# First four blocks in pairs with 384-byte load rows, headwise key-query products, late bias sum, fewer weight buffers

## Chip, cores, metric

One core of a Trainium2 chip. The metric is the device time of one execution in microseconds, median of several runs; every time is that of fast or undisturbed runs. TensorE is PE in the profile (PEld its weight loads), VectorE DVE, ScalarE ACT, GpSimd POOL, and SP the engine that issues the loads and stores.

## The reference, cut to what matters

```python
# gated linear attention; q, k, v, f_logit are 4 x 8 x 768 x 48 in float32
f = 1 / (1 + exp(-f_logit))
for t in range(S):
    state = f[:, :, t, :, None] * state + einsum('bhd,bhe->bhde', k[:, :, t], v[:, :, t])
    y[:, :, t] = einsum('bhd,bhde->bhe', q[:, :, t], state)
# y becomes x (3072 x 384), then a feed-forward layer with softplus
h = x @ w_in                                   # w_in  384 x 2048
g = maximum(h, 0) + log1p(exp(-abs(h)))
out = g @ w_out                                # w_out 2048 x 384
```

## The kernel before

The 3072 tokens are 24 blocks of 128. Per block: attention in chunk form (`zz`, `cs`, `ee`, `qkp`, `qkT`, `pp`, `ptm`, `uu`, `oo`, `xx`, `xT`), then `hh` = w_in times `xT`, exp and ln on ACT (`uexp`, `gg`), then `ops` = w_out times `gg`. Weights come in four quarters each, are cast to bf16, half on DVE and half on POOL.

Each piece of work is a task with an engine, an assumed cost, needs and perhaps a buffer. A list order walks through assumed time, picks the task that can start first, and writes it to its engine's queue. Each engine then works through its queue in that order.

```python
def in_order(tasks, slots):
    ...
        for e, waiting in queue.items():           # every engine, "DMA" and "SP" among them
            for t in waiting[:60]:                 # sorted by key
                r = ready(t)                       # None while a need or its buffer has no end yet
                ...
                if first is None or start < first[0] - 0.03:
                    first = (start, t)
...
    def load_w(n, w):
        ... t = work.tile([128, KT, WQ], FP32, name="w32", tag="w32", bufs=8)
...
    turn = blocks(0, 1, 2, 3) + [("wi", w) for w in range(4)] + [("wo", w) for w in range(4)]
    for kd, (n, i) in enumerate(turn):             # then the loads of blocks 4 on
        if n in SRC:
            task(("go", n, i), "SP", 0.5, [(used[n], i - LOADS)], kd, load, (n, i))
            task(("dma", n, i), "DMA", 1.04, [("go", n, i)], kd)
        else:
            task(("go", n, i), "SP", 0.5, [], kd, load_w, (n, i), "w32",
                 [("cast", n, i, 1), ...])         # the buffer is free after this cast
            task(("dma", n, i), "DMA", 2.3, [("go", n, i)], kd)
```

Two assumptions are to be kept in mind. An issue holds SP for 0.5 us whatever the transfer takes; and "DMA" takes its waiting transfers by key, that is in the order of `turn`, not in the order of issue.

Until about 24 us of assumed time, idle stretches of TensorE are filled with dummy matmuls (`ops<-negU,ident`), counted from the assumed start of the next real one.

```python
        each = 0.11 if start < WARM_FROM + 4 else 0.056
        for _ in range(int(max(0.0, start - idle_from - 0.1) / each * 0.9)):
            nc.tensor.matmul(...)                  # dummy
```

## Time and profile before

| | before |
|---|---|
| median of runs | 199.06 us (198.86 to 200.39) |
| span of the profiled run | 197.0 us |
| first `hh` | 24.72 us |
| w_out casts on DVE | 31.7, 34.2, 36.3, 38.4 us |
| TensorE without gaps from | 88 us |

The lines themselves stand in the prediction.

### The profile page before, as it was taken

The numbers are of one execution on the slowest core, as the hardware profiler recorded it, in microseconds if no ns is written. First come the engines' busy times: TensorE is split into PE (matmuls) and PEld (weight loads), VectorE is DVE, ScalarE is ACT, GpSimd is POOL, SyncE is SP. The second block draws the span as 40 slices with busy tenths as digits, with TensorE's granted clock in tenths as the row PEclk, the third lists the DMA queues.
The fourth block names the chain that finished last, engine by engine and source line by source line (L and its number), as shares of the span: only waits on it lengthen the run. The fifth ranks groups of instructions, "written<-read, shape, count | busy, mean of one in ns | idle before, by whom it ended". The sixth has DMA issues, their size and how long they took to land.

```text
span 197.0 us, 6209 instructions
## 1 busy us (share of the span) xinstructions
PE 184.4 (94%) x2491; PEld 152.7 (78%) x2491; DVE 142.9 (73%) x336; ACT 150.1 (76%) x251; POOL 98.1 (50%) x142
## 2 busy tenths in 40 slices
PE   6886997899999999989999999999999999999993
PEld 5775786666687888868888888888888888888872
DVE  6543774625999989999989889858778988773011
ACT  4566388886859996987989797898879778766770
POOL 2266867999997652652463364344246334500000
PEclk9999999999999999999999999999999999999998
DMA  6999999999999999999978757846541101102676
GB/s 124 188 189 176 352 382 374 244 198 187 188 165 194 186 190 173 277 195 208 233 146 172 144 118 160 161 113 137 113 90 41 42 2 43 40 29 75 163 188 171
DMA packets 109532, 32.34 MB, mean 164 GB/s; under 512 B 101184, under 2 KB 107968, under 8 KB 109504
## 3 DMA queue, kind: packets, MB, share of 16 engines
q1 hardware_dynamic: 109504, 31.96, 78.4%
q8 instruction: 19, 0.31, 0.7%
q14 instruction: 9, 0.07, 0.1%
HBM read 27.23 MB, written 4.72 MB: 162 GB/s over the span
## 4 chain that ended last, share of the span: by engine, by line
PE 57%; DVE 12%; SPq 10%; POOL 8%; DMA 6%; ACT 3%; issue 2%; ACTq 0%; POOLq 0%
PE hh L407 22%; PE ops L427 21%; SPq L140 8%; DMA w<-in_moe_w_out_dram 6%; POOL wsum L213 4%; PE qkT L268 3%; PE pp L303 3%; DVE ptm L315 3%; DVE ect L336 2%; POOL w_out_bf L191 2%; SPq L177 2%; PE oo L379 2%; DVE osb L458 1%; PE xTp L393 1%; PE ops L434 1%
## 5 line engine op out<-in xcount | busy, mean ns | idle before, releaser
L407 PE MATMUL hh<-xT,w_in_bf 128*128 128x128 bf16 x1152 | 112.3, 219 | 1.6 <-ACT uexp L415 0.9
L427 PE MATMUL ops<-w_out_bf,gg 128*128 128x384 bf16 x368 | 107.8, 326 | 1.0 <-POOL w_out_bf L191 0.9
L407 PEld LDWEIGHTS <-w_in_bf 128*128 128x128 bf16 x1152 | 88.0, 98 | 22.5 <-DVE xT L191 0.9
L415 ACT ACTIVATE uexp<-hh 128x512 f32<-128x512 f32 x96 | 56.5, 596 | 24.9 <-PE hh L407 24.1
L421 ACT ACTIVATE gg<-uexp 128x1024 bf16<-128x1024 f32 x48 | 50.7, 1056 | 1.4
L427 PEld LDWEIGHTS <-gg 128*128 128x128 bf16 x368 | 35.2, 98 | 5.3 <-issue 1.5
L363 POOL TENSOR_TENSOR sst<-tt,ect 48x192 bf16<-48x192 f32 x32 | 16.5, 517 | 31.7 <-DVE tt L354 25.5
L315 DVE TENSOR_TENSOR ptm<-pp,mask 128x512 bf16<-128x512 f32 x48 | 31.0, 684 | 1.6 <-PE pp L303 1.2
L250 POOL TENSOR_TENSOR qkp<-kk,ee 128x384 bf16<-128x384 f32 x23 | 21.1, 917 | 21.7 <-ACT ee L242 14.1
L191 DVE COPY qkT<-qkT 128x512 bf16<-128x512 bf16 x41 | 17.4, 423 | 13.8 <-PE qkT L268 9.6
L254 POOL TENSOR_TENSOR qkp<-qq,ee 128x384 bf16<-128x384 f32 x24 | 22.2, 924 | 0.3
L336 DVE STREAM_TRANSPOSE ect<-ee 32x128 bf16<-32x128 bf16 x64 | 19.5, 305 | 1.5
L191 POOL CAST vb<-vv 128x384 bf16<-128x384 f32 x24 | 12.6, 524 | 15.5 <-DMA vv<-in_v_dram 10.7
L229 ACT ACTIVATE ff<-ff 128x384 f32<-128x384 f32 x24 | 12.2, 516 | 7.0 <-DMA ff<-in_f_logit_dram 7.0
L454 DVE TENSOR_TENSOR osb<-ops,bias_bc 128x384 f32<-128x384 f32 x16 | 8.9, 556 | 9.4 <-PE ops L427 9.1
L618 PE MATMUL ops<-negU,ident 128*128 128x128 bf16 x169 | 13.9, 233 | 1.9 <-POOL ident masks.py:199 1.9
L213 POOL TENSOR_TENSOR wsum<-wsum,w 128x384 f32<-128x384 f32 x14 | 14.5, 1034 | 0.5
L191 DVE CAST xx<-oo 128x384 bf16<-128x384 f32 x21 | 11.7, 556 | 4.2 <-PE oo L379 3.9
L618 PEld LDWEIGHTS <-ident 128*128 128x128 bf16 x169 | 11.3, 105 | 4.4 <-issue 1.9
L242 ACT ACTIVATE ee<-cs 128x384 bf16<-128x384 f32 x24 | 11.5, 479 | 3.2 <-PE uu L323 1.7
L268 PE MATMUL qkT<-ident,qkp 128*128 128x128 bf16 x160 | 12.7, 219 | 1.0 <-POOL qkp L254 1.0
L303 PE MATMUL pp<-qbd,qkT 112*128 112x256 bf16 x80 | 12.9, 272 | 0.0
(60 smaller groups left out, 201.9 us busy)
## 6 DMA issues: line engine op xcount, KB each, us to landing
ff<-in_f_logit_dram SPq DMA_DIRECT2D x24, 192.0 KB, 4.5
kk<-in_k_dram SPq DMA_DIRECT2D x24, 192.0 KB, 4.4
qq<-in_q_dram SPq DMA_DIRECT2D x24, 192.0 KB, 4.2
vv<-in_v_dram SPq DMA_DIRECT2D x24, 192.0 KB, 4.4
out_dram<-osb SPq DMA_DIRECT2D x23, 192.0 KB, 2.4
w<-in_moe_w_in_dram SPq DMA_DIRECT2D x4, 768.0 KB, 8.6
w<-in_moe_w_out_dram SPq DMA_DIRECT2D x4, 768.0 KB, 12.7
rows<-in_q_dram SPq DMA_DIRECT2D x1, 1152.0 KB, 7.3
```

Source lines behind the costliest of these rows:

```text
L191: on[eng].tensor_copy(out=out, in_=in_)
L213: nc.gpsimd.tensor_tensor(out=wsum, in0=wsum, in1=t[:, j, :], op=ALU.add)
L250: on[eng].tensor_tensor(out=qkp_bufs[i % 3][:, H:2 * H, 0:D], in0=in_t.pop(("k", i)), in1=e_bufs[i % 2][:, H:2 * H, 0:D], op=ALU.mult)
L254: on[eng].tensor_tensor(out=qkp_bufs[i % 3][:, 0:H, 0:D], in0=in_t.pop(("q", i)), in1=e_bufs[i % 2][:, 0:H, 0:D], op=ALU.mult)
L303: nc.tensor.matmul(out=ps[:, u * 256:(u + 1) * 256], lhsT=qkT_t[i][0:112, NP + p, :], rhs=qbd_bufs[i % 2][0:112, p, :], start=True, stop=True,
L315: nc.vector.tensor_tensor(out=to, in0=p_ps.pop((i, half)).rearrange("p (a t) -> p a t", t=128), in1=mask4, op=ALU.mult)
L336: nc.vector.transpose(out=t[32 * r:32 * r + 32], in_=e[96:128, 0:NP, 32 * r:32 * r + 32])
L407: nc.tensor.matmul(out=h_ps[i, j // 4][:, j % 4, :], lhsT=w_in_bf[:, r, j * 128:(j + 1) * 128], rhs=xT_t[i][:, r, :], start=(r == 0), stop ...
L415: nc.scalar.activation(out=u_t[i, a // 2][:, 4 * (a % 2):4 * (a % 2) + 4, :], in_=h_ps.pop((i, a)), func=AF.Exp, bias=0.0, scale=1.0)
L421: nc.scalar.activation(out=g_t[i][:, 8 * a:8 * a + 8, :], in_=u_t.pop((i, a)), func=AF.Ln, bias=0.5, scale=0.5)
L427: nc.tensor.matmul(out=o_ps[i][:, 0:DM], lhsT=g_t[i][:, j, :], rhs=w_out_bf[:, j, :], start=(j == 0), stop=(j == NJ - 1), skip_group_check ...
L618: nc.tensor.matmul(out=idle_ps[:, 0:128], lhsT=ident, rhs=negU, start=True, stop=True, skip_group_check=True)
```

## The change

Its intent: longer load rows for the first four blocks so that the weights arrive sooner; fewer DVE copies; POOL freed of the bias sum while it is needed. The pairs and the 16 output buffers take SBUF, so the weights get five buffers in place of eight.

```diff
     def load(n, i):
+        if i < PAIRED:                       # PAIRED = 4; two tokens per partition
+            t = work.tile([128, H, 2, D], FP32, name=n + "2", tag=n + "2", bufs=2)
+            nc.sync.dma_start(out=t, in_=SRC[n][b, :, c * T:(c + 2) * T, :].rearrange(
+                "h (p e) d -> p h e d", e=2))
...
-            t = work.tile([128, KT, WQ], FP32, name="w32", tag="w32", bufs=8)
+            t = work.tile([128, KT, WQ], FP32, name="w32", tag="w32", bufs=5)
...
+    def a_cs2(i, e):                         # two matmuls, split sum
+    def a_p2(i, e, b):                       # 8 matmuls 48x64 x 48x128, four times a pair
+    def a_u2(i, n): ...                      # halved contractions
+    def a_o2(i, n): ...
...
-    def a_p(i, half):                        # 2 matmuls of 112 rows, 256 columns (qbd)
+    def a_p(i, b):                           # 4 matmuls of 48 rows, 128 columns, in all blocks
...
-        osb = work.tile([128, DM], FP32, name="osb", tag="osb", bufs=6)
+        osb = work.tile([128, DM], FP32, name="osb", tag="osb", bufs=16)
-        nc.vector.tensor_tensor(out=osb_t[i], in0=osb_t[i], in1=bias_bc, op=ALU.add)
+        nc.gpsimd.tensor_tensor(out=osb_t[i], in0=osb_t[i], in1=bias_bc, op=ALU.add)
...                                           # test loads in store() removed
-            task(("go", n, i), "SP", 0.5, [(used[n], i - LOADS)], kd, load, (n, i))
-            task(("dma", n, i), "DMA", 1.04, [("go", n, i)], kd)
+            task(("go", n, i), "SP", 0.55,
+                 [(used[n], i - LOADS) if i - LOADS >= PAIRED else None], kd, load, (n, i))
+            task(("dma", n, i), "DMA", 1.55 if i < PAIRED else 1.05, [("go", n, i)], kd)
...
-                 [("cast", n, i, 1), ("sum", 4 * i + 2) if n == "wo" else None])
+                 [("cast", n, i, 0), ("cast", n, i, 1), ("sum", 4 * i + 2) if n == "wo" else None])
...
-        task(("sum", n), "POOL", 0.91, [...], 40 + 3 * n, add_w, (w, j))
+        task(("sum", n), "POOL", 1.08, [...], SUMS + 8 * n, add_w, (w, j))
-    slots = dict(..., qkp=3, vb=3, qbd=2, w32=8, osb=6)
+    slots = dict(..., qkp=4, vb=4, qkT2=3, w32=5, osb=16)
```

## The prediction

> **What bounds the kernel now.** I read the page's engine shares first, then a table of busy time by stage, then the timelines of TensorE, the DMA-issuing queue and VectorE, and last what TensorE waited for.
>
> ```profile
> span 197.0 us, 6209 instructions
> ...
> PE 184.4 (94%) x2491; PEld 152.7 (78%) x2491; DVE 142.9 (73%) x336; ACT 150.1 (76%) x251; POOL 98.1 (50%) x142
> ...
> PE 57%; DVE 12%; SPq 10%; POOL 8%; DMA 6%; ACT 3%; issue 2%; ACTq 0%; POOLq 0%
> ```
>
> PE at 94% is not useful work: matmuls overlap, and 169 of them are dummies that keep the clock up before the real work. So I count real work by the distance between starts. In unbroken runs 24 `hh` matmuls take 1.34 us (0.0556 each), 8 `ops` 1.30 (0.163 each), and one block's attention needs transposes 0.45, `pp` 0.44, `oo` 0.37, `uu` 0.17, `xTp` 0.17, `cs` 0.16. By stage:
>
> ```profile
> 0.00:24.72 24.72, 19.27 (x303) 16.70 (x304) 13.98 (x38) 12.57 (x25) 13.21 (x26) 1.00 1.09 207
> 24.72:33.00 8.28, 6.99 (x122) 6.29 (x118) 5.65 (x10) 7.01 (x12) 5.06 (x7) 1.00 1.04 380
> 33.00:54.30 21.30, 19.97 (x210) 14.50 (x210) 12.30 (x25) 16.93 (x29) 20.69 (x24) 1.00 1.24 215
> 54.30:88.00 33.70, 32.62 (x456) 27.39 (x456) 32.04 (x79) 28.72 (x49) 21.05 (x31) 1.00 1.08 197
> 88.00:173.00 85.00, 85.00 (x1159) 71.04 (x1160) 71.98 (x172) 71.16 (x120) 38.14 (x57) 1.00 0.54 115
> ```
>
> The columns are stretch, length, busy PE, PEld, DVE, ACT, POOL, then clock, DMA share, GB/s. Four regimes: no `hh` at all until 24.72; POOL nearly full (20.7 of 21.3) until 54; DVE nearly full (32.0 of 33.7) until 88; then PE alone, with no gap. The first stage is set by the loads:
>
> ```profile
> 6.00:12.00 6.00, 5.29 (x94) 4.55 (x91) 3.76 (x10) 2.99 (x7) 3.11 (x5) 1.00 1.42 188
> 21.00:36.00 15.00, 13.23 (x211) 11.24 (x209) 10.00 (x18) 10.36 (x16) 11.00 (x14) 1.00 1.04 372
> ...
> 178.25:178.50 0.25, 1.00 1.08 292
> 178.50:178.75 0.25, 1.00 1.15 321
> ```
>
> ```profile
> 12.98 2.22 SPq L140 DMA_DIRECT2D kk<-in_k_dram  x1
> ...
> 16.87 3.62 SPq L177 DMA_DIRECT2D w<-in_moe_w_in_dram  x4
> ...
> 23.19 0.69 DVE L191 CAST w_in_bf<-w 128x768 bf16<-128x768 f32 x1 [0.50 <-DMA w<-in_moe_w_in_dram]
> ...
> 24.72 1.50 PE L407 MATMUL hh<-xT,w_in_bf 128*128 128x128 bf16 x24
> ```
>
> Sixteen loads of 192-byte rows go ahead of the weights at 188 GB/s, 1.04 us each; weights with long rows then run at 372. The first weight quarter is cast at 23.19 and `hh` starts when both halves are cast. Block 0's `xT` had been ready since 14.2, so weights, not attention, start the feed-forward part. The two lines from 178 us (stretch, length, clock, DMA share, GB/s) are a small load of 384-byte rows that the old kernel happens to make near its end.
>
> What TensorE then waited for (24.7 to 90):
>
> ```profile
> PE qkT L268 <- POOL qkp L254: 1.0, 3, 0.5
> PE hh L407 <- ACT uexp L415: 0.9, 2, 0.7
> PE ops L427 <- POOL w_out_bf L191: 0.9, 3, 0.3
> PE hh L407 <- DVE xT L191: 0.6, 1, 0.6
> ```
>
> **What the Trainium skill says.**
> - "DMA: Bandwidth & Descriptors", Specifications, wants rows of at least 512 B for line rate, and its section on small descriptors names a fixed cost per descriptor. The trace agrees: 188 GB/s at 192 B, 372 at 1.5 to 2 KB, about 300 at 384 B.
> - "TensorEngine Tiling (Array Packing)", Key Properties: tiles of the array work independently, but changing the tiling mode drains it. The trace shows both: eight K=48 `pp` matmuls start about 27 ns apart, but the next full-array matmul comes 0.35 us after the first.
> - "Perfetto Trace Analysis", Optimizing Scalar/DVE Operations: each vector instruction pays a fixed access cost, more from PSUM, so fewer and larger ones help. Here `qkT` copies of 384 and 512 columns take 351 and 423 ns (the first is `xT`): 72 ns per 128 columns, so over 130 ns are fixed.
> - "SBUF — State Buffer", Who interferes with whom: VectorE and GpSimd block each other on a shared port. Here the `w_out_bf` cast on DVE takes 0.56 us alone and up to 1.23 beside POOL's sums.
>
> **The change part by part.**
>
> 1. *Pairs for blocks 0 to 3, 384-byte rows.* Eight loads of 384 KB in place of sixteen of 192 KB. Estimate of one: per engine a 192-byte descriptor takes 16.2 ns (1.04 us over 64) and a 2,048-byte one 88 ns (372 GB/s over 16), so a line through both gives 23.6 ns at 384 B, 1.51 us a load; the small load near the end ran at about 300 GB/s, 1.31 us. I take 1.41: 11.3 us against 16.6. The weights arrive 5.3 us earlier, and `hh` starts at about 19.4 if `xT` of block 0 is there. It should be: the first `ff` pair lands 0.7 us later than now (4.5), four activations of 0.52 to 6.6, `cs` and four exponentials of 0.48 to 9.0, the second `qkp` on POOL to 10, transposes and a wide eviction to 11.5, products and four masks of 0.68 to 14.6, then `oo`, `xx`, `xTp`, `xT` to about 16.5. So the path is −5.3.
>    The pairs add PE work (two-matmul `cs`, 32 products in place of 16, halved contractions in `uu` and `oo`): some 1.3 us a pair. For pair 0 this lies in idle time; of pair 1 I put +1.2 on the path, since more of it now comes after `hh` starts.
> 2. *Headwise products everywhere.* For 20 blocks the three `qkT`/`qbd` copies and the k copy (start to start 0.34 + 0.42 + 0.46 + 0.34 = 1.56 us) become one of 1,024 columns, estimated 423 + 4 × 72 = 711 ns. DVE: −0.85 × 20 = −17 us of busy time, but on the path only where DVE set the pace, 54 to 88. On PE, four matmuls of 256 columns (0.44) become eight of K=48 (0.35 with the drain behind; a drain ahead may add 0.1): −0.1 to 0 per block, −1.0 in all.
> 3. *Bias sum late.* The 15 sums of about 1.03 us leave POOL's stretch from 33 to 49.5, where the timeline shows 4.23 us of them directly before block 4's first `qkp` at 45.28; the casts of `w_out` no longer queue behind them. The seven adds on DVE (0.6 us each, 4.2) go, and 13 adds of about 1 us come to POOL late, where it is under half busy.
> 4. *The lost TensorE time.* Work from 24.72 to the end: 1152 × 0.0556 + 368 × 0.163 + 2.65 (last halves) + 33.9 (attention of 20 blocks, fewer `uu` and state products in first and last chunks) + 0.9 + 0.6 (bias) = 162.1. PE's last matmul starts its end at 193.57, so 168.85 − 162.1 = 6.7 us are lost, nearly all before 88 (the four waits above, 3.4, and the pipeline refill behind each gap). Parts 2 and 3 remove the waits on POOL and DVE: I take −3.0. The ACT waits stay: one block's `exp` and `ln` need 4 × 0.60 + 2 × 1.06 = 4.5 us against 2.67 of `hh`.
> 5. *Fewer load buffers (3 for 4), 5 weight buffers for 8, no test loads near the end*: nothing. The last store landed in 1.9 us beside them, no later than stores usually do (2.4).
>
> Sum: −5.3 + 1.2 − 1.0 − 3.0 = −8.1; 199.2 − 8.1 = 191.1. I say 191.4, as waits are more often moved than removed.
>
> **The rivals.**
> - *The head is bound elsewhere.* Pair 0 needs both halves of f before either `cs`, and all masks before `oo`; if that chain is 3 us longer than my count, it sets `hh` in place of the weights. For: four masks and wide evictions in series on DVE. Against: 3 us of slack. It would leave −2 to −3 of part 1: about 194.
> - *The drain eats part 2.* If the two halves of `pp` are separated by other matmuls, each pays a drain: 0.32 us for four K=48 in the trace (22.75 to 23.07), so 0.64 against 0.44, +4 us over 20 blocks: 195 to 196. Against: from 88 on, the four `pp` come together in nearly every block.
> - *Block 4 comes late.* PE ran out of `ops` of blocks 0 to 3 at 53.6 and got block 4's `hh` at 54.27. If PE starts 5.3 earlier but block 4, behind all weights in the queue, doesn't, PE idles: up to +2. Against: its loads too move up by what the pairs save, and POOL is free for it.
> - *The late sums hold an output.* From block 13 on outputs need the bias, and there are two `ops` banks: a late sum stops PE. Against: POOL then has 3.5 us of work in a 6.9 us block.
>
> **Range and chances.** Head −4.0 to −6.2, lost time −0.5 to −4.5, `pp` −2 to +2, pair extras +0.5 to +2. They are hardly linked, so 188.3 to 195.0 should hold 8 times in 10. Faster by over 2% means under 195.2: 0.90; within 2%: 0.08; slower: 0.02.
>
> **What would show it.** Right: `hh` starts near 19.4 directly after the first `w_in` cast; eight early loads about 1.4 us apart; POOL's `qkp` of block 4 not behind sums; DVE clearly below 90% from 50 to 85; PE without gaps from about 45; a steady block of 6.8 to 6.9 us (6.92 now, `oo` to `oo`); last `ops` near 186. Wrong: `hh` waiting for `xT` in the head; `pp` taking over 0.5 us a block; a gap before block 4; a stop before the output of block 13.

## More of the kernel before

The experiments ran in three sets of rounds (e1 to e4, e5 to e8, e9 to e11), each set on another chip and each with the kernel before beside it; across sets the ratios are the better comparison.

One more view of the kernel before is needed for the comparison: the SP queue after the w_in quarters (start, length, what).

```profile
20.54 7.39 SPq L182 DMA_DIRECT2D w<-in_moe_w_out_dram  x4
28.04 1.51 SPq L140 DMA_DIRECT2D ff<-in_f_logit_dram  x1
```

All four w_out quarters are issued together, directly behind w_in; the first load of block 4 stands behind them.

## The result

The changed kernel took 207.92 us (206.95 to 208.74, 4 runs) against 199.06: ratio 1.0428, 95% interval 1.0363 to 1.0493, slower. (A ratio is the mean time of one kernel's fast runs over that of the other's of the same rounds, so not quite the ratio of the medians.) The page after:

```profile
span 205.9 us, 6423 instructions
...
PE 190.4 (92%) x2646; PEld 154.9 (75%) x2646; DVE 125.5 (61%) x274; ACT 149.4 (73%) x249; POOL 109.4 (53%) x154
...
PE   6999985069999999999999999999999999999994
...
PEclk9999999757999999999999999999999999999999
```

PE shows a hole in the eighth slice of 40 (36 to 41 us), and the clock granted to TensorE falls with it. DVE lost 17.4 us of busy time (parts 2 and 3 of the prediction had 17 + 4.2; the difference was not traced), and the total is still longer. The stages, in the same stretches as before:

```profile
24.72:33.00 8.28, 7.54 (x146) 6.37 (x145) 4.59 (x9) 6.38 (x10) 5.79 (x8) 1.00 1.03 194
33.00:54.30 21.30, 11.71 (x104) 8.45 (x102) 4.75 (x11) 7.96 (x15) 10.38 (x11) 0.76 0.65 173
54.30:88.00 33.70, 33.70 (x478) 26.82 (x476) 26.29 (x58) 29.10 (x50) 25.65 (x37) 1.00 0.81 153
```

From 54 on PE is full, where before it was full from 88: that part of the aim was reached. But between 33 and 54 it is busy for 11.7 of 21.3 us, and from 36 to 42 every other engine is idle too. What each was waiting for, first PE and then DVE (a bracket gives the idle time just before and its releaser):

```profile
33.30 0.33 PE L494 MATMUL ops<-w_out_bf,gg 128*128 128x384 bf16 x1
43.22 0.50 PE L460 MATMUL xTp<-ident,xx 128*128 128x128 bf16 x3 [9.59 <-DVE xx L211]
...
44.48 1.49 PE L494 MATMUL ops<-w_out_bf,gg 128*128 128x384 bf16 x4
```

```profile
42.14 0.56 DVE L211 CAST w_out_bf<-w 128x768 bf16<-128x768 f32 x1 [11.68 <-DMA w<-in_moe_w_out_dram]
42.62 0.55 DVE L211 CAST xx<-oo 128x384 bf16<-128x384 f32 x1
```

TensorE waits 9.6 us for the copy `xx` of block 3. That copy stands in DVE's queue behind the cast of w_out's second quarter, and the cast waits 11.7 us for the weight. After the gap four `ops` matmuls take 1.28 us to the next start, 0.32 each, twice the 0.163 of a warm stream: the clock was at 0.57 between 40 and 50. Why the weight is late stands in the SP queue:

```profile
14.88 1.19 SPq L202 DMA_DIRECT2D w<-in_moe_w_out_dram  x1
16.11 1.75 SPq L146 DMA_DIRECT2D ff<-in_f_logit_dram  x1
17.89 4.95 SPq L146 DMA_DIRECT2D kk<-in_k_dram  x1
...
35.19 0.65 SPq L146 DMA_DIRECT2D vv<-in_v_dram  x1
35.97 2.13 SPq L202 DMA_DIRECT2D w<-in_moe_w_out_dram  x3
```

One w_out quarter is issued at 14.88; then twelve loads of blocks 4, 5 and 6; and only at 35.97 the other three quarters. One of the issues took 4.95 us: it held SP while the weights ahead of it were still moving (about 390 GB/s from 18 to 24 us). So nothing more of w_out was in place before 42. The buffer was not what held it: both casts of the first w_in quarter had ended by 20.3 (DVE, 19.34 + 0.99), and the trace shows no wait of SP for a buffer before 48. The buffer stood free for over 15 us while SP worked through the twelve loads.

**Theory 1.** With five buffers a w_out quarter must wait for a w_in buffer. In the list order its task was not ready, twelve input loads were, and an issue was assumed to cost 0.55 us; the order also assumed that the weights' transfers, by their lower key, overtake loads already issued. So it placed the three quarters behind twelve loads and believed them early. The chip's queue keeps the order of issue. **Rivals:** the copy's place in DVE's queue alone (2); five buffers being too few in themselves (3); the pairs, headwise products or late sums (4); the slower head of the changed kernel (5: too many dummies ahead of the first `cs`, or the weights' casts).

### The profile page after: what moved, and what is told of

Read it like the earlier page. It is cut to its first block, busy times and chain, and to the rows that moved or that the text cites. A ratio compares the mean times of both kernels' runs of the same rounds, so it can differ in the third digit from the quotient of the medians.

```text
span 205.9 us, 6423 instructions
## 1 busy us (share of the span) xinstructions
PE 190.4 (92%) x2646; PEld 154.9 (75%) x2646; DVE 125.5 (61%) x274; ACT 149.4 (73%) x249; POOL 109.4 (53%) x154
## 4 chain that ended last, share of the span: by engine, by line
PE 78%; SPq 17%; DMA 3%; issue 1%; DVE 0%
PE ops L494 30%; PE hh L474 29%; SPq L146 9%; SPq L141 5%; PE qkT L296 4%; PE pp L374 4%; DMA w<-in_moe_w_out_dram 3%; SPq L197 2%; PE oo L446 2%; PE xTp L460 2%; PE cs L257 2%; PE oo L441 1%; PE uu L391 1%; PE ops L501 1%; SPq L202 1%
## 5 line engine op out<-in xcount | busy, mean ns | idle before, releaser
L474 PE MATMUL hh<-xT,w_in_bf 128*128 128x128 bf16 x1152 | 113.9, 220 | 0.7 <-ACT uexp L482 0.7
L494 PE MATMUL ops<-w_out_bf,gg 128*128 128x384 bf16 x368 | 109.4, 332 | 0.0
L383 DVE TENSOR_TENSOR ptm<-pp,mask 128x512 bf16<-128x512 f32 x40 | 25.9, 686 | 9.1 <-PE pp L374 9.0
L278 POOL TENSOR_TENSOR qkp<-kk,ee 128x384 bf16<-128x384 f32 x20 | 18.3, 915 | 19.7 <-issue 12.9
L211 DVE COPY qkT<-qkT 128x1024 bf16<-128x1024 bf16 x22 | 15.2, 691 | 17.3 <-PE qkT L296 16.6
L282 POOL TENSOR_TENSOR qkp<-qq,ee 128x384 bf16<-128x384 f32 x20 | 18.3, 916 | 0.0
L460 PE MATMUL xTp<-ident,xx 128*128 128x128 bf16 x72 | 8.1, 223 | 9.6 <-DVE xx L211 9.6
L211 DVE CAST xx<-oo 128x384 bf16<-128x384 f32 x21 | 11.7, 557 | 6.5 <-PE oo L446 6.1
L525 POOL TENSOR_TENSOR osb<-osb,bias_bc 128x384 f32<-128x384 f32 x13 | 12.6, 1003 | 0.9 <-DVE bias_bc L243 0.9
L460 PEld LDWEIGHTS <-xx 128*128 128x128 bf16 x72 | 5.1, 99 | 10.1 <-DVE xx L211 9.9
L521 DVE TENSOR_TENSOR osb<-ops,bias_bc 128x384 f32<-128x384 f32 x10 | 5.6, 558 | 10.4 <-PE ops L494 10.3
```

What stands on the lines that cost most here:

```text
L211: on[eng].tensor_copy(out=out, in_=in_)
L278: on[eng].tensor_tensor(out=qkp_bufs[i % 4][:, H:2 * H, 0:D], in0=in_t.pop(("k", i)), in1=e_bufs[i % 2][:, H:2 * H, 0:D], op=ALU.mult)
L282: on[eng].tensor_tensor(out=qkp_bufs[i % 4][:, 0:H, 0:D], in0=in_t.pop(("q", i)), in1=e_bufs[i % 2][:, 0:H, 0:D], op=ALU.mult)
L383: nc.vector.tensor_tensor(out=ptm_t[i].rearrange("p (a b) t -> p b a t", b=2)[:, half, :, :], in0=p_ps.pop((i, half)).rearrange("p (a t) - ...
L474: nc.tensor.matmul(out=h_ps[i, j // 4][:, j % 4, :], lhsT=w_in_bf[:, r, j * 128:(j + 1) * 128], rhs=xT_t[i][:, r, :], start=(r == 0), stop ...
L494: nc.tensor.matmul(out=o_ps[i][:, 0:DM], lhsT=g_t[i][:, j, :], rhs=w_out_bf[:, j, :], start=(j == 0), stop=(j == NJ - 1), skip_group_check ...
```

## The experiments

Eleven kernels ran. All gave correct results. Each ratio is to the kernel before in the same rounds.

| run | edit | median us | ratio (95% interval) |
|---|---|---|---|
| e1 | changed, w_out issued ahead of block 4 | 195.08 | 0.977 (0.974 to 0.981) |
| e2 | changed, late casts off DVE | 206.34 | 1.033 (1.029 to 1.038) |
| e3 | before, five weight buffers | 215.69 | 1.081 (1.076 to 1.086) |
| e4 | changed, fewer dummies | 206.63 | 1.036 (1.031 to 1.040) |
| e5 | e1 and e4 | 195.01 | 0.979 (0.977 to 0.980) |
| e6 | before, headwise only | 202.05 | 1.016 (1.013 to 1.018) |
| e7 | before, late bias only | 198.06 | 0.993 (0.992 to 0.994) |
| e8 | before, e6 and e7 | 197.07 | 0.989 (0.988 to 0.990) |
| e9 | e5, weights assumed 3 us later | 194.16 | 0.973 (0.971 to 0.975) |
| e10 | e4, list order told of the queue | 194.37 (one of six runs, 198.05, was slow and is left out) | 0.975 (0.972 to 0.978) |
| e11 | e9 with one pair only | 195.73 | 0.982 (0.979 to 0.985) |

### e1: the order of loads

```diff
-                 [(used[n], i - LOADS) if i - LOADS >= PAIRED else None], kd, load, (n, i))
+                 [(used[n], i - LOADS) if i - LOADS >= PAIRED else None,
+                  ("go", "wo", 3) if i >= PAIRED else None], kd, load, (n, i))
```

> Changed kernel, one edit: the loads of blocks 4 and later are issued only after all four w_out quarters (still five weight buffers). Theory 1 (load order: with five buffers the list order put twelve input loads ahead of the last three w_out quarters, which then land at 42 us): the 9.6 us gap of TensorE before 43.2 and the cold clock behind it vanish, about 9.6 + 2.9 = 12.5 us less, so 194 to 197. Rival 2 (VectorE's in-order queue is what counts): the same gain. Rival 3 (five buffers are too few by themselves, the queue now stalls for a free buffer and starves block 4): gain under 5 us, over 202.

Measured 195.08, 12.8 less than the changed kernel, all of what was expected. Of TensorE's waits only small ones in the head are left (total, times, longest):

```profile
PE hh L474 <- ACT uexp L482: 0.7, 2, 0.6
PE qkT L305 <- DVE qkp L278: 0.2, 1, 0.2
```

There are still five buffers, so rival 3 falls. The queue does stall for a free buffer (5.1 of the 9.85 us of the four w_out issues are waits for casts of w_in), but the weights ahead keep the transfers going: 372 to 396 GB/s from 18 to 30 us. Rival 2 expected the same gain and is left to e2.

### e2: the cast's place in DVE's queue

```diff
-ON = {}
+ON = {("cast", "wo", w, 0): "POOL" for w in range(1, 4)}
```

> Changed kernel, load order as it is, but VectorE's halves of the casts of the late three w_out quarters moved to GpSimd, so that the copy xx of block 3 no longer stands behind a late cast on VectorE. Theory 1 (the late weights themselves): TensorE gets block 3's hh early (2.7 us of work) but no ops, so at most 3 to 4 us less: 204 to 207. Rival 2 (only the place in VectorE's queue): 8 us or more less, under 200.

Measured 206.34, within theory 1's range. The copy came early, TensorE did block 3's `hh` at 33.0, and then stood for the weight itself:

```profile
PE ops L494 <- POOL w_out_bf L211: 10.4, 1, 10.4
```

Rival 2 falls: the queue on DVE chose the name of the wait, not its length.

### e3: five buffers in the kernel before

```diff
-            t = work.tile([128, KT, WQ], FP32, name="w32", tag="w32", bufs=8)
+            t = work.tile([128, KT, WQ], FP32, name="w32", tag="w32", bufs=5)
...
-    slots = dict(..., w32=8, ...)
+    slots = dict(..., w32=5, ...)
```

> The kernel before with five weight buffers for eight, nothing else (its list order then puts sixteen input loads ahead of the last three w_out quarters). Theory 1: a gap of TensorE in the 30s and 40s as in the changed kernel, 6 to 14 us slower than before, 205 to 213. Rival 4 (the pairs, the headwise products or the late sums make the loss): within 1 us of before.

Measured 215.69, 16.1 above the kernel before: the direction is right, the size is past my range. Sixteen loads (there are four load buffers) went ahead of the last three quarters, which were issued at 45.05:

```profile
52.02 1.44 PE L427 MATMUL ops<-w_out_bf,gg 128*128 128x384 bf16 x4 [15.66 <-POOL w_out_bf L191]
```

This part of the diff alone, in a kernel without any other part of the change, makes a loss of this kind. Rival 4 is not needed for it. That the changed kernel loses less (8.9 us) fits its faster head and its twelve loads for sixteen; this was not tested apart.

### e4: fewer dummies

TensorE reached the first `cs` at 9.06 us though `zz` was ready at 6.4: the rule above counts 0.056 us for each dummy once the assumed start is past 5.6, and the 80 took 7.2 us, 0.09 each.

```diff
-                each = 0.11 if start < WARM_FROM + 4 else 0.056
+                each = 0.11 if idle_from < WARM_FROM + 4 else 0.056
```

> Changed kernel, load order as it is; only the number of warm-up matmuls ahead of the first cs is cut (about 40 for 80), since TensorE was still working them off at 9.06 us though zz was ready at 6.4. Theory 1: hh starts 2 us earlier but the w_out quarters still land at 42, so the end moves by under 1 us: 207 to 208.5. Rival 5 (the head's delay carries through to the end): 205 to 206.

`cs` came at 6.11 and `hh` at 19.65 in place of 21.41. Measured 206.63, a little under my range; its interval overlaps that of the changed kernel (1.036 and 1.043), so whether 1 us was gained is not settled. What sets the end moved little: the second w_out quarter is cast at 41.22 in place of 42.14. The result lies between the two ranges, so neither theory met its own.

### e5: right order and fewer dummies

> Changed kernel with both edits: input loads of block 4 on behind all weights, and about 40 warm-up matmuls for 80 ahead of the first cs. Theory 1: with the gap gone TensorE is packed from 32 us on, so the 1.8 us that hh starts earlier (19.4 for 21.2) now reach the end: 192.8 to 194. Rival 5 (weights, not xT, hold hh from 19.4 on; or ACT fills up): under 0.7 us less than with the load order alone, over 194.4.

A miss of theory 1: 195.01, the same as e1. `hh` starts 1.5 us earlier than in e1, but from 22.2 on the two traces run alike. GpSimd's queue shows why (start, length, what, idle before):

```profile
15.09 0.96 POOL L211 CAST vb<-v 128x384 bf16<-128x384 f32 x2 [0.94 <-DMA v<-in_v_dram]
18.46 1.08 POOL L211 CAST w_in_bf<-w 128x768 bf16<-128x768 f32 x1 [2.41 <-DMA w<-in_moe_w_in_dram]
...
20.97 1.84 POOL L282 TENSOR_TENSOR qkp<-q,ee 128x384 bf16<-128x384 f32 x2
```

The q products of blocks 2 and 3 stand behind a w_in cast that waits for its weight, and TensorE waited 1.3 us for them (2.5 us for `qkp` in all; the other 1.2 belong to the first pair, before `hh` starts). That is most of the 1.5 us. The time of the first `hh` is not the time from which it can run on. GpSimd's casts of the second and third w_in quarters stand behind those products (at 22.76), so `hh` could not go past the first quarter of the first two blocks before then; the next `hh` after that quarter starts at 24.29.

### e6, e7, e8: the other parts alone, in the kernel before

```diff
 # e6
-HEADWISE = 4
-ON = {}
+HEADWISE = 24
+ON = {("evq", i): "DVE" for i in range(4, 24)}
 # e6 has two copies of 512 columns a block, where the changed kernel has one of 1,024
 # e7: the late-bias lines of the diff above (LATE = 13, 16 output buffers, adds on GpSimd,
 #     sums spread late), test loads removed; eight weight buffers
 # e8: e6 and e7 together
```

> The kernel before with only the headwise products in all blocks (q and k copies of 512 columns both on VectorE, no qbd copies). Theory A (the drain ahead and behind eats the concurrency: a packed TensorE block stays at 6.98 us; VectorE's relief only removes the waits of 54 to 88): 197.5 to 199.2. Rival B (each block 0.1 us shorter on TensorE besides): 195.5 to 197.5.

> The kernel before with only the bias sum spread late, adds on GpSimd, 13 late outputs, 16 output buffers, and without the test loads near its end. Theory A (GpSimd's sums held block 4's qkp and the w_out casts): 1 to 2.5 us less, 196.7 to 198.2. Rival B (those waits were filled anyway by other blocks' ops): within 0.7 us of before.

> The kernel before with both, headwise products and late bias sum, eight weight buffers, no pairs. Theory A: the two gains add up to what I took for the lost time, 3 us, so 195.5 to 197.5; the pairs with the right load order and dummies are worth the rest down to 193. Rival B (the pairs are all of the gain): over 198.

e7 gained 1.2 us (low end of theory A; some 0.3 of it may be the test loads, without which the last store lands in 1.6 us in place of 1.9), e8 2.2 (theory A). e6 is a miss of both theories: 202.05, 1.6% slower. Its trace has a cold stretch (clock 0.56 and 0.58 from 20 to 24 us, behind a wait of 1.4 us that the kernel before has too) and 1.8 us of waits for ACT at 94.6 and 96.9; together with the later first `hh` (25.42) this covers the 2.4 us by which the profiled span is longer, but its runs were longer still, and why is open. With the late bias the same edit gains 1 us (e7 to e8), so the products themselves do not cost it; that the list order does is likely, but not shown.

What a packed block pays for headwise products is read from e8, 117.6 to 118.8:

```profile
117.97 0.33 PE L408 MATMUL hh<-xT,w_in_bf 128*128 128x128 bf16 x3
118.23 0.41 PE L294 MATMUL pp<-qkT 48*128 48x128 bf16 x8
118.57 0.34 PE L428 MATMUL ops<-w_out_bf,gg 128*128 128x384 bf16 x1
118.75 0.22 PE L408 MATMUL hh<-xT,w_in_bf 128*128 128x128 bf16 x1
```

Three `hh` take 0.167, so without a drain `pp` would start at 118.14: 0.09 ahead of it; 0.34 to the next start; and that `ops` is 0.015 longer than usual. Sum 0.445 us, against 0.43 for the four wide products before (113.23 to 113.66 there). The concurrency is real and the two drains take all of it. A block stays at 7.04 us from `pp` to `pp` (111.19 to 118.23), as before (113.23 to 120.27).

### e9, e10, e11: the order told the truth, and one pair only

```diff
 # e9 (on top of e5)
-            task(("at", n, i), None, 1.9, [("dma", n, i)], 0)
+            task(("at", n, i), None, 4.9, [("dma", n, i)], 0)
 # e10 (on top of e4; no order imposed)
+            task(("go", n, i), "SP", 1.45 if i < PAIRED else 1.05, ...)     # 2.1 for a weight
+            task(("dma", n, i), None, 0.1, [("go", n, i)], kd)
 # e11 (on top of e9)
-PAIRED = 4
+PAIRED = 2
```

> Changed kernel with the right load order and fewer dummies, and one number of its list order besides: weights are assumed to land 3 us later, so that GpSimd's queue has the q products of blocks 2 and 3 ahead of the first w_in cast (in the run before it stood 2.4 us waiting for that weight, and TensorE then 2.5 us for the products). Theory 1 (in-order queues of the head pass the wait on): 193.0 to 194.3, TensorE's wait for qkp in the head gone. Rival 5 (hh quarters are held by the weight casts themselves): within 0.5 us of 195.0.

194.16, as theory 1 said: TensorE's wait for the q products of blocks 2 and 3 is gone (1.2 us for the first pair's are left), and the kernel beats e5 by 0.9 us, though its `hh` starts 2.6 us later (22.24). The edit reorders every queue of the head, so that the gain comes from this wait alone is not shown. It has the lowest median, 5.4 us under the kernel before in its rounds; the ratio of e10 lies inside its interval.

> Changed kernel with fewer dummies, five weight buffers, no order imposed; instead the list order is told that a load holds the issuing queue for its transfer's time (1.45, 1.05, 2.1 us) in place of 0.5 and of a transfer queue that takes the weights first. Theory 1 (the wrong order came from that picture of the queue, not from five buffers): all four w_out quarters stand ahead of block 4's loads, no gap of TensorE over 2 us, 194 to 196.5. Rival 3 (five buffers are the fault): over 200.

194.37. Nothing was imposed; once the list order knew that an issue holds the queue, it put all four w_out quarters ahead of block 4 by itself (SP queue):

```profile
13.59 11.38 SPq L202 DMA_DIRECT2D w<-in_moe_w_out_dram  x4
25.02 0.51 SPq L146 DMA_DIRECT2D ff<-in_f_logit_dram  x1
```

This shows the cause of the wrong order, with five buffers. The run corrects two assumptions at once. The list order can be worked out from the kernel's code without a run: with the issue times alone put right, all four quarters also come ahead of block 4, so the assumed 0.55 us of a load is enough to make the wrong order.

> As the run with late weights in the list order, but only blocks 0 and 1 as a pair; blocks 2 and 3 are loaded singly with 192-byte rows. Theory 6 (the second pair's extra TensorE work, some 2.5 us more than two plain blocks after hh has started, is what I undersized): the loads cost 8.3 for 5.8 us, so hh starts 2.5 us later, and TensorE does 2.5 us less: within 1 us of the run with two pairs. Rival 7 (only the weights' arrival counts): 2 to 2.5 us slower than with two pairs.

195.73, 1.6 above e9, between the two: the second pair brings `hh` 2.9 us sooner (22.24 against 25.11) and gives back part of it in TensorE work.

## Why the prediction was wrong

- **The step that failed** is part 5, "5 weight buffers for 8 ...: nothing". I asked how much the buffers hold and not what the list order does when a buffer isn't free. e3 prices the step alone at +16.1 us, e1 takes 12.8 back out of the changed kernel. The rival "block 4 comes late" looked at the same queue from the wrong side: block 4's loads came too early.
- **Part 1, the loads:** the pair loads were issued 1.48 us apart (estimate 1.41; the line through two row lengths had given 1.51, the small load 1.31), and the weights were cast from 18.2 (23.2 before). Right. My 16.5 for `xT` was not: in the changed kernel it held `hh` until 21.41, as the first rival had it, because of the dummies. e4 brings `hh` to 19.65 (predicted 19.4), but that nearness is luck: even there `xT` came only at 19.6 (its copy starts at 19.11 and takes 0.5), 3 us after my count and just behind the last cast of the first w_in quarter (18.34 + 1.08). e5 shows that this start alone is worth nothing.
- **Part 1, the pairs' extra work:** too small. In e5 TensorE spends 4.8 us on pair 1 after `hh` has begun (transposes 0.8, `uu` 1.1, `pp` 1.0, `oo` 1.6, `xTp` 0.3, start to start); my sum had 0.9 + 1.2.
- **Part 2, headwise:** −1.0 predicted, 0 measured: both drains are always paid. My own "−0.1 to 0 per block" had the answer at its end. The wide copy took 691 ns (estimate 711): DVE's relief was right.
- **Part 3, late sums:** right in kind; alone −1.2 us (e7), with the headwise edit −2.2 (e8), where I had put −3.0 for the waits of POOL and DVE.
- **The sum without the failed step:** e5 has its last output operation at 190.27 us; the path had 193.57 − 8.1 = 185.5. Of the 4.8 us between, 0.25 are the start of `hh`, 1.0 the products, 2.7 the pair, and some 0.8 are left for lost time. So even with the loads in order my 191.4 was too low, and 195.0 was at the edge of the range.
- **The clock** I left out: about 2.9 us of the loss is TensorE at half speed (0.54 from 43.2 to 49.0) behind the gap.
- **A reading of the lines** that was wrong: the `w_out_bf` cast of 0.56 us (31.71) did not run alone. POOL's cast stood beside it (31.74) and took 1.22 us, against 0.82 for the one at 40.31.

## What to carry to other kernels

When a change takes buffers away from loads, read the program order of the issuing queue before judging it free: a load that isn't ready lets others pass, and in a queue that keeps the order of issue they stay ahead. A list order needs a true picture of the queue (in these traces an issue into a backed-up queue holds it for about the transfer's time, and what is issued later stays behind), or it will place waits in every engine's queue that follows. And an earlier start of the first matmul is only worth what the next inputs behind it allow.

## What the Trainium skill lacked or had wrong

- "DMA: Bandwidth & Descriptors", Issuing engines are not separate DMA queues, calls the sequencer's time to initiate a DMA usually small relative to the DMA. Here an issue lasted as long as its transfer as soon as the queue was backed up: 1.44 us for each pair load, and 4.95 for one small load behind the weights. The skill gives no duration for an issue into a backed-up queue.
- The same page has no rate on this chip for loads with rows between 192 and 512 B: 384 KB in 384-byte rows came every 1.48 us, and the trace shows 261 GB/s (4.45 to 8.90 us), against 188 GB/s at 192 B.
- "TensorEngine Tiling (Array Packing)", Key Properties, names the drain on a change of tiling mode without its size. In e8 entering cost 0.09 us, and eight concurrent K=48 products with both drains 0.445 us against 0.43 for four full-width ones of the same result.
